# Retention and a feed-forward block on one core: queries loaded with four tokens on a partition, outputs scaled in the order of the result, and keys 6 transposed by the DMA queue

## The chip, the cores and the metric

The kernel runs on one core of one Trainium2 chip. The metric is the device time of one execution in microseconds (us), from the runs' own clock; the profile is taken in an execution of its own, and its span, from the first to the last instruction, is a little shorter.

A core has a matrix engine (TensorE; PE in the profile, PEld for its weight loads), three engines for elementwise work (VectorE = DVE, ScalarE = ACT, GpSimd = POOL), and a queue engine (SyncE = SP) that here issues nearly all DMA transfers. Sixteen DMA engines carry them out. SBUF is the memory on the core, PSUM the memory that TensorE writes its products into.

## The reference

The first half is a recurrent form of attention over a sequence of 768 tokens, for 4 batches and 8 heads of 64; its result goes through a feed-forward block with a product in the middle.

```python
# q, k, v: (4, 8, 768, 64)
gamma = 1 - 2 ** (-5 - arange(H))              # one decay for each head
for t in range(S):
    state = gamma * state + k[t] v[t]^T         # 64 x 64 for each batch and head
    y[t]  = scale * q[t] @ state
x = y.transpose(0, 2, 1, 3).reshape(B * S, H * D)        # (3072, 512)
a = x @ w1;  b = x @ w2                                  # (3072, 1024)
out = ((a * b) @ w3) @ w_out                             # (3072, 512)
```

## The kernel before

The work is cut into 12 steps, `m` = 0 to 11. A step takes 128 tokens (a chunk) of two batches; six chunks make up a sequence, so steps 0 to 5 belong to the first two batches and 6 to 11 to the other two. In a chunk the two halves of 64 tokens are `s` = 0 and 1. The heads come in four pairs `p`, with `r` for the head in the pair and `e` for the batch. Steps 0 and 1 have a form of their own (class `Pairs`), in which each of the two takes 256 tokens of one batch.

For each step the kernel multiplies keys by queries (`scores`), masks the result, multiplies it by the values (`intra`), adds the product of the queries with the state (`inter`), scales the sum by the decays (`outputs_back`), and carries the state on (`kv`). Step `m` also runs the feed-forward block of `m - 1` and its last product for `m - 2`. w3 and w_out have been multiplied into one matrix at the start.

TensorE needs queries and keys with the 64 elements of a head on the partitions. They come from memory with tokens on the partitions, are cast to 16 bits, and are then transposed, either by TensorE with a copy out of PSUM (`k_transposes`) or by a DMA transpose (`k_dma`, `q_dma`).

```python
wstage = ctx.enter_context(tc.tile_pool(name="wstage", bufs=22))
ps_f   = ctx.enter_context(tc.tile_pool(name="ps_f", bufs=4, space=PSUM))

def load_q(n):                         # 256 tokens of one batch, all heads
    g, e = divmod(n, 2)
    if g >= NSTEP // 2:
        return
    bp, cp = divmod(g, NCH // 2)
    q_in[n] = load_pairs(q, bp * 2 + e, cp)

def load_pairs(src, b, cp):            # two tokens on a partition: runs of 2 x 64 x 4 bytes
    t = new_stage()
    dma_in(
        t[:, :].rearrange("p (h x) -> p h x", x=2 * D),
        src[b, :, cp * 2 * C : (cp + 1) * 2 * C, :].rearrange("h (p t) d -> p h (t d)", t=2),
    )
    return t
...
def pairs_cast(dst, src, *engs):
    n = H // len(engs)
    for i, eng in enumerate(engs):
        hs = slice(i * n, i * n + n)
        (nc.scalar.copy if eng is nc.scalar else eng.tensor_copy)(
            dst[:, :].rearrange("i (t h d) -> i h t d", t=2, d=D)[:, hs, :, :],
            src[:, :].rearrange("i (h t d) -> i h t d", t=2, d=D)[:, hs, :, :],
        )
...
def q_dma(n):
    qT = att.tile([128, 2, NP, 128], HP, tag="qT", name="qT", bufs=5)
    nc.sync.dma_start_transpose(
        qT[:, :, :, :].rearrange("p t a i -> p (t a) i"), q16s.pop(n)[:, :]
    )
    qTs[n] = qT

def k_transposes(m, tag):              # eight transposes on TensorE, one copy on VectorE
    k16, kT = k16s[m], new_kT(m)
    ...
    for e in range(2):
        for p in range(NP):
            nc.tensor.transpose(ps[:, e, p, :], k16[:, e, p * 128 : (p + 1) * 128], ident16[:, :])
    nc.vector.tensor_copy(kT..., ps...)

def k_dma(m):
    nc.sync.dma_start_transpose(new_kT(m)..., k16s[m]...)

def queries(m, e, p, s, r):
    c = m % NCH
    i0 = c % 2 * 64 + s * 32
    return qTs[m // 2 * 2 + e][half(r), :, p, i0 : i0 + 32]      # 2 runs of 32 columns

def scores(m, engs=None):
    ...
                    nc.tensor.matmul(
                        ps[r][half(s), p * 2 + e, :], lhsT=kT[half(r), e, p, half(s)],
                        rhs=queries(m, e, p, s, r), start=True, stop=True,
                    )
    def back(r):                       # "am_back": the mask, on VectorE
        nc.vector.tensor_tensor(
            am[:, r, :, :], ps[r][:, :, :],
            keep[:, :].unsqueeze(1).broadcast_to((128, NP * 2, L)), MULT,
        )
...
def ended(mm, eng=None):               # a tiny copy that ends after mm
    mark = (eng.tensor_copy if eng else nc.scalar.copy)(mark_t[:, :], Z[0:1, 0:1])
    wait_for(mark, mm)
    return mark

def outputs_back(m, s):                # XT = psY * YS, tokens in natural order in XT
    swap = s == 1 and m % NCH > 0
    for to in (half(0), half(1)) if swap else (slice(0, 128),):
        fr = half(1 - to.start // L) if swap else to
        n = fr.stop - fr.start
        nc.vector.tensor_tensor(
            XT[m][to, :, s, :].rearrange("p (a e) (i t) -> p a e t i", e=2, t=2),
            psYs[m][s][fr, :, :].rearrange("p (a e) (t i) -> p a e t i", e=2, t=2),
            YS[fr, s + swap, :, :].unsqueeze(2).broadcast_to((n, NP, 2, L))
            .rearrange("p a e (t i) -> p a e t i", t=2),
            MULT,
        )
```

The products in PSUM have their 64 columns in the order of the query columns, all tokens with t = 0 first and then those with t = 1; XT has them in the order of the tokens.

The steps from 3 on, in the order in which each engine is given its instructions:

```python
EARLY = (6, 11, 12)        # intra(m - 1) already in step m - 1
K_PE = (3, 5)              # steps in which the next keys are transposed by TensorE

def step(m):
    kv_backs = []
    if m > 4:
        last = None if m in EARLY else ended(intra(m - 1))
        if m < NSTEP:
            kv_backs.append(kv(m, True))
            am_back = scores(m)
        inter(m - 1, last)
    ...
    outputs_back(m - 1, 0)
    outputs_back(m - 1, 1)
    if m >= NSTEP:
        return
    if m + 1 < NSTEP:
        k_cast(m + 1, (nc.gpsimd, nc.gpsimd))
        if m not in K_PE:
            k_dma(m + 1)
    for kv_back in kv_backs:
        kv_back(0)
        kv_back(1)
    am_back(0)
    am_back(1)
    ffn[m - 2].o_unit(0)               # 8 products of 512 columns each, and the store
    ffn[m - 2].o_unit(1)
    load_q(m + 3) if m % 2 == 0 else None
    load_k(m + 2)
    load_v(m + 2)
    load_q(m + 3) if m % 2 else None
    for f in range(2):
        ffn[m - 1].ab(f)               # 8 products of 256 columns, ScalarE copies a, VectorE multiplies
    if m + 1 in EARLY:
        intra(m)
    if m + 1 < NSTEP:
        v_cast(m + 1, (nc.gpsimd, nc.gpsimd))
    ...
    ffn[m - 1].ab(2)
    ffn[m - 1].ab(3)
    ...
    if m % 2 == 0:
        for n in (m + 2, m + 3):
            q_cast(n, nc.gpsimd)
        for n in (m + 2, m + 3):
            q_dma(n)
    for f in range(4, 8):
        if f == 6 and m in K_PE:
            k_transposes(m + 1, None)
        ffn[m - 1].ab(f)
```

Of the kernel before, what the change touches and what calls it, by code (L numbers as in the profile page):

```python
# [12 lines left out]
MULT = mybir.AluOpType.mult  # L13
# [5 lines left out]
def kernel(  # L19
# [11 lines left out]
    nc = tc.nc  # L31
    B, H, S, D = q.shape
    C = 128
    L = 64
    WST = 22
    NCH = S // C
# [4 lines left out]
    TB = 256  # L41
    K_PE = 4

# [15 lines left out]
    def half(x):  # L59
        return slice(x * L, (x + 1) * L)  # L60

    def dma_in(dst, src):
        nc.sync.dma_start(dst, src)  # L63
# [5 lines left out]
    q_in, k_in, v_in = {}, {}, {}  # L69

    def load_q(n):

        g, e = divmod(n, 2)
        if g >= NSTEP // 2:
            return
        bp, cp = divmod(g, NCH // 2)
        q_in[n] = load_pairs(q, bp * 2 + e, cp)

    def load_pairs(src, b, cp):
        t = new_stage()  # L80
# [5 lines that stand above are left out]
# [19 lines left out]
    def new_stage():  # L105
        return wstage.tile([128, 1024], FP, tag="wst", name="stg")
# [18 lines left out]
    for f in range(4, 8):  # L125
        w3_st.append(load_rows(moe_w3, f))
    for e in range(2):
        load_q(e)
        k_in[e] = load_pairs(k, e, 0)
        v_in[e] = load_pairs(v, e, 0)  # L130
    w1_st = [load_rows(moe_w1, d) for d in range(4)]
# [19 lines left out]
    for s in range(2):  # L151
        nc.gpsimd.iota(ip_i[half(s), 0:2, :], pattern=[[1, 2], [0, H]], base=1, channel_multiplier=2)
    if_i = const.tile([128, 2, L], mybir.dt.int32, name="if_i")
    nc.gpsimd.iota(if_i[:, :, :], pattern=[[L, 2], [1, 2], [2, 32]], base=1, channel_multiplier=0)
    LGH = const.tile([128, H], FP, name="LGH")
    LGP = const.tile([128, 2, NP], FP, name="LGP")
    for h in range(H):
# [2 lines left out]
    YS = const.tile([128, 3, NP, L], FP, name="YS")  # L160
# [12 lines left out]
    def masks_and_decays():  # L173

        nc.gpsimd.memset(keep[:, :], 1.0)
        for s in range(2):
            r = slice(s * L, (s + 1) * L)
            nc.gpsimd.affine_select(
                out=keep[r, :], in_=keep[r, :], compare_op=mybir.AluOpType.is_ge, fill=0.0,
                base=0, pattern=[[1, 2], [2, 32]], channel_multiplier=-1,  # L180
            )

        nc.gpsimd.memset(keep_t[:, :, :], 1.0)
        for s in range(2):
            for t in range(2):
                nc.gpsimd.affine_select(
                    out=keep_t[half(s), t, :], in_=keep_t[half(s), t, :], compare_op=mybir.AluOpType.is_ge,
                    fill=0.0, base=-t, pattern=[[1, 2], [2, 64]], channel_multiplier=-2,
                )
        for h in range(H):  # L190
            for s in range(2):
                nc.gpsimd.memset(LGP[half((h + s) % 2), s, h // 2 : h // 2 + 1], math.log(gam[h]))
        for h in range(H):
            p, r = h // 2, (h % 2) * 64
            nc.gpsimd.memset(GS[r : r + 64, p : p + 1], gam[h] ** C)
# [11 lines left out]
    XT = {}  # L207
# [70 lines left out]
    q16s, k16s, v16s, qTs, kTs, AMs, psYs, Ts = {}, {}, {}, {}, {}, {}, {}, {}  # L278

    def q_cast(n, *engs):  # L280
        if n not in q_in:
            return
        q16s[n] = att.tile([128, 1024], HP, tag="q16", name="q16", bufs=2)
        pairs_cast(q16s[n], q_in.pop(n), *engs)

    def pairs_cast(dst, src, *engs):
        n = H // len(engs)
        for i, eng in enumerate(engs):
            hs = slice(i * n, i * n + n)
            (nc.scalar.copy if eng is nc.scalar else eng.tensor_copy)(  # L290
                dst[:, :].rearrange("i (t h d) -> i h t d", t=2, d=D)[:, hs, :, :],
                src[:, :].rearrange("i (h t d) -> i h t d", t=2, d=D)[:, hs, :, :],
            )

    def k_cast(m, engs):
        k16 = att.tile([128, 2, 512], HP, tag="k16", name="k16", bufs=3)
        k32 = k_in.pop(m)
        if len(engs) == 1:
            parts = [(k16[:, :, :].rearrange("p e x -> p (e x)"), k32[:, :, :].rearrange("p e x -> p (e x)"))]
        else:  # L300
            parts = [(k16[:, e, :], k32[:, e, :]) for e in range(2)]
        for eng, (dst, src) in zip(engs, parts):
            (nc.scalar.copy if eng is nc.scalar else eng.tensor_copy)(dst, src)  # L303
        k16s[m] = k16
# [57 lines left out]
    def k_dma(m):  # L362
        nc.sync.dma_start_transpose(
            new_kT(m)[:, :, :, :].rearrange("p e a j -> p (e a) j"),
            k16s[m][:, :, :].rearrange("p e x -> p (e x)"),
        )

    def queries(m, e, p, s, r):
        c = m % NCH
        i0 = c % 2 * 64 + s * 32  # L370
        return qTs[m // 2 * 2 + e][half(r), :, p, i0 : i0 + 32]

# [22 lines left out]
    class Pairs:  # L397
# [4 lines left out]

        def k_cast(self, *engs):
            self.k16 = att.tile([128, 1024], HP, tag="k16", name="k16", bufs=3)
            pairs_cast(self.k16, k_in.pop(self.e), *engs)

        def k_transposes(self, tag, on_dve, parts=1):
            self.kT = att.tile([128, 2, NP, 128], HP, tag="kT", name="kT", bufs=2)
# [9 lines left out]
            )  # L418

        def queries(self, r, p, s):  # L420
            return qTs[self.e][half(r), :, p, half(s)]

        def scores(self, t):
            am = att.tile([128, 2, NP, 128], HP, tag="am", name="am")
# [18 lines left out]
        def intra(self, t):  # L443
            if t == 0:
                self.y = [bank(f"Y{s}", [128, NP, 128], FP, "psY") for s in range(2)]
            for p in range(NP):
                for s in range(2):
                    for r in range(2):
                        c0 = p * 128 + r * 64
                        last = nc.tensor.matmul(  # L450
                            self.y[s][half(r), p, :], lhsT=self.v16[half(s), t, c0 : c0 + 64],
                            rhs=self.am[t][half(s), r, p, :], start=(t == 0 and p == 0),
                            stop=(s == 0 and t == 1 and p == NP - 1),
                        )
            return last
# [50 lines left out]
        def outputs_back(self, s):  # L506
            if self.e not in XT:
                XT[self.e] = xpool.tile([128, NP * 2, 2, L], HP, tag="xt", name="xt")
            nc.vector.tensor_tensor(
                XT[self.e][:, :, :, :].rearrange("p (a s) b x -> p a s (b x)", s=2)[:, :, s, :]  # L510
                .rearrange("p a (b i t) -> p a t b i", b=2, t=2),
                self.y[s][:, :, :].rearrange("p a (t b i) -> p a t b i", t=2, b=2),
                YS[:, 0:2, :, :].rearrange("p b a (t i) -> p a t b i", t=2), MULT,
            )


# [68 lines left out]
    def ended(mm, eng=None):  # L585
# [4 lines that stand above are left out]
# [17 lines left out]
    def outputs_back(m, s):  # L607
        if m not in XT:
            XT[m] = xpool.tile([128, NP * 2, 2, L], HP, tag="xt", name="xt")
        swap = s == 1 and m % NCH > 0  # L610
        for to in (half(0), half(1)) if swap else (slice(0, 128),):
            fr = half(1 - to.start // L) if swap else to
            n = fr.stop - fr.start
            nc.vector.tensor_tensor(  # L614
                XT[m][to, :, s, :].rearrange("p (a e) (i t) -> p a e t i", e=2, t=2),
                psYs[m][s][fr, :, :].rearrange("p (a e) (t i) -> p a e t i", e=2, t=2),
                YS[fr, s + swap, :, :].unsqueeze(2).broadcast_to((n, NP, 2, L))
                .rearrange("p a e (t i) -> p a e t i", t=2),
                MULT,
            )  # L620

# [89 lines left out]
    w3_part(2, 1, 2)  # L711
    cast_wo(3)
    masks_and_decays()
    cast_w3(4)
    for f in range(3):
# [12 lines left out]
    wb.mm(4)  # L728
    wb.back()
    q_cast(0, nc.gpsimd)  # L730
    wb = W3Block(5)
    wb.mm(4)
# [22 lines left out]
    am_back(1)  # L755
    b0.intra(0)
    q_cast(1, nc.scalar, nc.gpsimd)
    wb.mm(1)
    q_transposes(1, "X0", False)
# [81 lines left out]
    q_cast(3, nc.gpsimd)  # L841
    q_transposes(2, "X0", False)
    k_cast(2, (nc.gpsimd, nc.scalar))
    v_cast(2, (nc.gpsimd, nc.gpsimd))
    for f in range(2):
# [27 lines left out]

    EARLY = (6, 11, 12)

    K_PE = (3, 5)

    def step(m):  # L880

# [4 lines that stand above are left out]
# [12 lines left out]
# [4 lines that stand above are left out]
# [11 lines left out]
# [4 lines that stand above are left out]
# [15 lines left out]
# [3 lines that stand above are left out]
# [43 lines left out]
```

## Time and profile before

| | before |
|---|---|
| time, median of 3 runs | 184.48 us (184.39 to 185.63) |
| span of the profiled execution | 181.5 us |
| TensorE busy | 175.3 us |
| VectorE busy | 108.6 us |
| ScalarE, GpSimd busy | 71.9, 71.3 us |
| DMA packets, data | 79,531, 39.71 MB |

The page of a profile gives the busy time of each engine and a row of 40 slices of the span, each digit the busy share in tenths. The chain of work that ended last follows back from the last instruction what released each piece of work, so that its pieces fill the span. Groups of instructions bear the line of the kernel that issued them (L614 is line 614), their shapes, the busy time, and the mean duration of one. A line with SPq is the time in which the queue engine was issuing a transfer, not the transfer itself; "to landing" is the time from an issue to the arrival of its data.

### The profile page before, as it was taken

The numbers are of one execution on the slowest core, as the hardware profiler recorded it, in microseconds if no ns is written. First come the engines' busy times: TensorE is split into PE (matmuls) and PEld (weight loads), VectorE is DVE, ScalarE is ACT, GpSimd is POOL, SyncE is SP. The second block draws the span as 40 slices with busy tenths as digits, with TensorE's granted clock in tenths as the row PEclk, the third lists the DMA queues.
The fourth block names the chain that finished last, engine by engine and source line by source line (L and its number), as shares of the span: only waits on it lengthen the run. The fifth ranks groups of instructions, "written<-read, shape, count | busy, mean of one in ns | idle before, by whom it ended". The sixth has DMA issues, their size and how long they took to land.

```text
span 181.5 us, 6220 instructions
## 1 busy us (share of the span) xinstructions
PE 175.3 (97%) x2634; PEld 125.4 (69%) x2634; DVE 108.6 (60%) x204; ACT 71.9 (40%) x156; POOL 71.3 (39%) x127
## 2 busy tenths in 40 slices
PE   7889999999999999999999999999999999999992
PEld 2445656688766785876967858768688587685871
DVE  1246658751769669558477584494674956745430
ACT  3354845555631341524334424244243332442431
POOL 3127536964537752725427273055460350000000
PEclk9999999999999999999999999999999999999999
DMA  5999999999999999999999999999999940201203
GB/s 204 376 417 401 298 291 350 409 371 242 194 256 226 182 301 211 203 312 198 245 202 198 295 169 244 190 208 265 236 114 261 178 149 4 116 0 42 78 0 116
DMA packets 79531, 39.71 MB, mean 219 GB/s; under 512 B 57361, under 2 KB 74001, under 8 KB 79505
## 3 DMA queue, kind: packets, MB, share of 16 engines
q1 hardware_dynamic: 79072, 38.81, 88.6%
q8 instruction: 20, 0.33, 0.8%
q10 hardware_dynamic: 432, 0.52, 0.8%
q14 instruction: 7, 0.05, 0.1%
HBM read 29.36 MB, written 6.29 MB: 196 GB/s over the span
## 4 chain that ended last, share of the span: by engine, by line
PE 88%; DMA 5%; ACT 2%; SPq 1%; DVE 1%; issue 0%; ACTq 0%
PE psF L636 41%; PE psO L663 23%; DMA stg<-in_moe_w_out_dram 5%; PE psF L795 4%; PE psW L269 3%; PE psW L255 3%; PE psY L531 2%; PE psY L599 2%; PE psA L383 2%; PE psG L636 2%; PE psK L551 2%; PE psTq L328 1%; PE psW L244 1%; SPq L63 1%; PE psTk L357 1%; PE psY L450 1%
## 5 line engine op out<-in xcount | busy, mean ns | idle before, releaser
L636 PE MATMUL psF<-xt,w 128*128 128x256 f16 x672 | 76.7, 273 | 0.0
L636 PEld LDWEIGHTS <-w 128*128 128x128 f16 x704 | 68.4, 98 | 10.3
L651 DVE TENSOR_TENSOR ht<-pa,psF 128x256 f16<-128x256 f32 x88 | 36.9, 420 | 37.6 <-PE psF L636 32.0
L645 ACT COPY pa<-psF 128x256 f32<-128x256 f32 x80 | 29.8, 373 | 37.5 <-PE psF L636 37.5
L663 PE MATMUL psO<-w3o,ht 128*128 128x512 f16 (+2 forms) x200 | 43.9, 371 | 0.0
L667 ACT ACTIVATE osb<-psO 128x512 f32<-128x512 f32 (+2 forms) x25 | 14.5, 581 | 44.0 <-PE psO L663 44.0
L663 PEld LDWEIGHTS <-ht 128*128 128x128 f16 x200 | 18.5, 98 | 19.4
L614 DVE TENSOR_TENSOR xt<-psY,YS 64x512 f16<-64x512 f32 (+1 forms) x29 | 21.1, 727 | 4.8 <-PE psY L599 4.4
L310 POOL TENSOR_TENSOR v<-stg,VS 128x512 f16<-128x512 f32 x20 | 20.6, 1042 | 5.4 <-DMA stg<-in_v_dram 5.4
L303 POOL CAST k<-stg 128x512 f16<-128x512 f32 x18 | 11.0, 612 | 26.1 <-DMA stg<-in_k_dram 25.9
L290 POOL CAST q<-stg 128x1024 f16<-128x1024 f32 (+1 forms) x12 | 12.0, 1003 | 17.9 <-DMA stg<-in_q_dram 13.8
L390 DVE TENSOR_TENSOR am<-psA,keep 128x512 f16<-128x512 f32 x20 | 12.8, 682 | 0.6 <-PE psA L383 0.6
L566 POOL TENSOR_TENSOR t<-s,GS 128x512 f16<-128x512 f32 x8 | 8.3, 1039 | 7.8 <-DVE s L565 7.8
L248 DVE COPY w3t<-psW 128x1024 f16<-128x1024 f16 x8 | 5.5, 690 | 5.3 <-PE psW L244 5.3
L269 PE MATMUL psW<-wo,w3t 128*128 128x512 f16 x32 | 8.6, 381 | 0.0
L255 PE MATMUL psW<-wo,w3t 128*128 128x512 f16 x32 | 8.0, 387 | 0.7 <-ACT wo L224 0.5
L795 PE MATMUL psF<-xt,w 128*128 128x256 f16 x64 | 8.3, 273 | 0.2
L686 PE MATMUL psZ<-zeros 128*128 128x512 f16 (+1 forms) x18 | 6.6, 504 | 1.3 <-DVE zeros L143 1.3
L795 PEld LDWEIGHTS <-w 128*128 128x128 f16 x64 | 5.8, 98 | 1.8 <-ACT w L769 0.6
L573 DVE TENSOR_TENSOR t<-psK,t 128x512 f16<-128x512 f32 x9 | 6.2, 690 | 0.6 <-PE psK L551 0.5
L244 PEld LDWEIGHTS <-w3h 128*128 128x128 f16 x64 | 4.4, 103 | 3.1 <-DVE w3h L231 1.7
L225 POOL CAST wo<-stg 128x512 f16<-128x512 f32 x4 | 2.5, 613 | 10.2 <-DMA stg<-in_moe_w_out_dram 10.2
(92 smaller groups left out, 149.3 us busy)
## 6 DMA issues: line engine op xcount, KB each, us to landing
stg<-in_moe_w_dram SPq DMA_DIRECT2D x16, 512.0 KB, 8.8
stg<-in_q_dram SPq DMA_DIRECT2D x12, 512.0 KB, 6.4
out_dram<-osb SPq DMA_DIRECT2D x22, 256.0 KB, 3.3
stg<-in_k_dram SPq DMA_DIRECT2D x20, 256.0 KB, 5.6
stg<-in_v_dram SPq DMA_DIRECT2D x20, 256.0 KB, 5.6
stg<-in_moe_w_out_dram SPq DMA_DIRECT2D x4, 512.0 KB, 7.9
stg<-in_k_dram SPq DMA_DIRECT2D x2, 512.0 KB, 9.5
stg<-in_v_dram SPq DMA_DIRECT2D x2, 512.0 KB, 8.6
```

The source lines that it names most:

```text
L255: nc.tensor.matmul(acc[f], lhsT=w3t[f][:, g * 128 : (g + 1) * 128], rhs=WO[i][:, r, :], start=(g == 0), stop=(g == 7),)
L269: nc.tensor.matmul(self.ps[:, :], lhsT=self.t[:, g * 128 : (g + 1) * 128], rhs=WO[g // 2][:, g % 2, :], start=(g == 0), stop=(g == 7),)
L290: (nc.scalar.copy if eng is nc.scalar else eng.tensor_copy)(dst[:, :].rearrange("i (t h d) -> i h t d", t=2, d=D)[:, hs, :, :], src[:, :]. ...
L310: eng.tensor_tensor(v16[:, e, :].rearrange("j (h d) -> j h d", d=D), v32[:, e, :].rearrange("j (h d) -> j h d", d=D), VS[:, 2, :].unsqueez ...
L390: nc.vector.tensor_tensor(am[:, r, :, :], ps[r][:, :, :], keep[:, :].unsqueeze(1).broadcast_to((128, NP * 2, L)), MULT,)
L614: nc.vector.tensor_tensor(XT[m][to, :, s, :].rearrange("p (a e) (i t) -> p a e t i", e=2, t=2), psYs[m][s][fr, :, :].rearrange("p (a e) (t ...
L636: nc.tensor.matmul(ps[:, :], lhsT=W[d][:, f * 128 : (f + 1) * 128], rhs=self.x(d), start=(d == 0), stop=(d == 3),)
L645: nc.scalar.copy(self.pa[f][:, :], ps[:, :])
L651: nc.vector.tensor_tensor(self.HT[:, f, :], self.pa.pop(f)[:, :], ps[:, :], MULT)
L663: nc.tensor.matmul(psO[:, :], lhsT=self.HT[:, f, e * 128 : (e + 1) * 128], rhs=W3O[f][:, cs], start=(f == 0), stop=(f == 7),)
L667: nc.scalar.activation(osb[:, cs], psO[:, :], AF.Copy, scale=final_scale)
L795: nc.tensor.matmul(ps[f // 2][:, f % 2, :], lhsT=W[d][:, f * 128 : (f + 1) * 128], rhs=f0.x(d), start=(d == 0 and f % 2 == 0), stop=(d == ...
```

## The change

There are three parts to it. Queries of steps 2 to 11 are loaded with four tokens on a partition instead of two, so that a run in memory is 1,024 bytes long instead of 512. A tile then holds four heads of both batches, 64 partitions each, and is loaded by two transfers of half the size. The cast, the masks and the query columns follow this order: a product's 64 columns now are 4 runs of 16. Steps 0 and 1 keep loading two tokens on a partition, and take their query columns with a step of two so that they come in the same order.

Second, `outputs_back` goes through its elements in the order of the result (i, then t): XT and the decays are now gone through without gaps, and the products in PSUM with a step of 16 elements from one to the next. Before, it went through the products without gaps, and wrote XT with a step of two.

Third, the keys of step 6 are transposed by the DMA queue in step 5, where TensorE did it before; and the early `intra` is that of step 7 (in step 7, ahead of step 8) in place of that of step 10 (ahead of step 11). The aim of the change is to take work from TensorE's list, with room for it in the DMA engines made by longer runs.

```diff
--- before.py
+++ after.py
@@ -70,11 +70,17 @@
 
     def load_q(n):
 
-        g, e = divmod(n, 2)
+        g, hh = divmod(n, 2)
         if g >= NSTEP // 2:
             return
         bp, cp = divmod(g, NCH // 2)
-        q_in[n] = load_pairs(q, bp * 2 + e, cp)
+        q_in[n] = new_stage()
+        for e in range(2):
+            dma_in(
+                q_in[n][half(e), :].rearrange("p (h x) -> p h x", h=4),
+                q[bp * 2 + e, hh * 4 : hh * 4 + 4, cp * 2 * C : (cp + 1) * 2 * C, :]
+                .rearrange("h (p t) d -> p h (t d)", t=4),
+            )
 
     def load_pairs(src, b, cp):
         t = new_stage()
@@ -125,7 +131,7 @@
     for f in range(4, 8):
         w3_st.append(load_rows(moe_w3, f))
     for e in range(2):
-        load_q(e)
+        q_in[e] = load_pairs(q, e, 0)
         k_in[e] = load_pairs(k, e, 0)
         v_in[e] = load_pairs(v, e, 0)
     w1_st = [load_rows(moe_w1, d) for d in range(4)]
@@ -151,7 +157,7 @@
     for s in range(2):
         nc.gpsimd.iota(ip_i[half(s), 0:2, :], pattern=[[1, 2], [0, H]], base=1, channel_multiplier=2)
     if_i = const.tile([128, 2, L], mybir.dt.int32, name="if_i")
-    nc.gpsimd.iota(if_i[:, :, :], pattern=[[L, 2], [1, 2], [2, 32]], base=1, channel_multiplier=0)
+    nc.gpsimd.iota(if_i[:, :, :], pattern=[[L, 2], [1, L]], base=1, channel_multiplier=0)
     LGH = const.tile([128, H], FP, name="LGH")
     LGP = const.tile([128, 2, NP], FP, name="LGP")
     for h in range(H):
@@ -177,7 +183,7 @@
             r = slice(s * L, (s + 1) * L)
             nc.gpsimd.affine_select(
                 out=keep[r, :], in_=keep[r, :], compare_op=mybir.AluOpType.is_ge, fill=0.0,
-                base=0, pattern=[[1, 2], [2, 32]], channel_multiplier=-1,
+                base=0, pattern=[[1, 4], [4, 16]], channel_multiplier=-1,
             )
 
         nc.gpsimd.memset(keep_t[:, :, :], 1.0)
@@ -185,7 +191,7 @@
             for t in range(2):
                 nc.gpsimd.affine_select(
                     out=keep_t[half(s), t, :], in_=keep_t[half(s), t, :], compare_op=mybir.AluOpType.is_ge,
-                    fill=0.0, base=-t, pattern=[[1, 2], [2, 64]], channel_multiplier=-2,
+                    fill=0.0, base=-t, pattern=[[1, 4], [4, 32]], channel_multiplier=-2,
                 )
         for h in range(H):
             for s in range(2):
@@ -281,15 +287,15 @@
         if n not in q_in:
             return
         q16s[n] = att.tile([128, 1024], HP, tag="q16", name="q16", bufs=2)
-        pairs_cast(q16s[n], q_in.pop(n), *engs)
-
-    def pairs_cast(dst, src, *engs):
-        n = H // len(engs)
+        token_cast(q16s[n], q_in.pop(n), 2 if n < 2 else 4, *engs)
+
+    def token_cast(dst, src, t, *engs):
+        n = 1024 // D // t // len(engs)
         for i, eng in enumerate(engs):
             hs = slice(i * n, i * n + n)
             (nc.scalar.copy if eng is nc.scalar else eng.tensor_copy)(
-                dst[:, :].rearrange("i (t h d) -> i h t d", t=2, d=D)[:, hs, :, :],
-                src[:, :].rearrange("i (h t d) -> i h t d", t=2, d=D)[:, hs, :, :],
+                dst[:, :].rearrange("i (t h d) -> i h t d", t=t, d=D)[:, hs, :, :],
+                src[:, :].rearrange("i (h t d) -> i h t d", t=t, d=D)[:, hs, :, :],
             )
 
     def k_cast(m, engs):
@@ -366,9 +372,9 @@
         )
 
     def queries(m, e, p, s, r):
-        c = m % NCH
-        i0 = c % 2 * 64 + s * 32
-        return qTs[m // 2 * 2 + e][half(r), :, p, i0 : i0 + 32]
+        qT = qTs[m // 2 * 2 + p // 2][half(r), :, :, :].rearrange("p t a i -> p (t a) i")
+        i0 = e * 64 + m % NCH % 2 * 32 + s * 16
+        return qT[:, p % 2 : 8 : 2, i0 : i0 + 16]
 
 
 
@@ -402,7 +408,7 @@
 
         def k_cast(self, *engs):
             self.k16 = att.tile([128, 1024], HP, tag="k16", name="k16", bufs=3)
-            pairs_cast(self.k16, k_in.pop(self.e), *engs)
+            token_cast(self.k16, k_in.pop(self.e), 2, *engs)
 
         def k_transposes(self, tag, on_dve, parts=1):
             self.kT = att.tile([128, 2, NP, 128], HP, tag="kT", name="kT", bufs=2)
@@ -418,7 +424,7 @@
             )
 
         def queries(self, r, p, s):
-            return qTs[self.e][half(r), :, p, half(s)]
+            return qTs[self.e][half(r), :, p, half(s)].rearrange("d t (i u) -> d u t i", u=2)
 
         def scores(self, t):
             am = att.tile([128, 2, NP, 128], HP, tag="am", name="am")
@@ -508,9 +514,9 @@
                 XT[self.e] = xpool.tile([128, NP * 2, 2, L], HP, tag="xt", name="xt")
             nc.vector.tensor_tensor(
                 XT[self.e][:, :, :, :].rearrange("p (a s) b x -> p a s (b x)", s=2)[:, :, s, :]
-                .rearrange("p a (b i t) -> p a t b i", b=2, t=2),
-                self.y[s][:, :, :].rearrange("p a (t b i) -> p a t b i", t=2, b=2),
-                YS[:, 0:2, :, :].rearrange("p b a (t i) -> p a t b i", t=2), MULT,
+                .rearrange("p a (b i t) -> p a b i t", b=2, t=4),
+                self.y[s][:, :, :].rearrange("p a (t b i) -> p a b i t", t=4, b=2),
+                YS[:, 0:2, :, :].rearrange("p b a (i t) -> p a b i t", t=4), MULT,
             )
 
 
@@ -612,10 +618,10 @@
             fr = half(1 - to.start // L) if swap else to
             n = fr.stop - fr.start
             nc.vector.tensor_tensor(
-                XT[m][to, :, s, :].rearrange("p (a e) (i t) -> p a e t i", e=2, t=2),
-                psYs[m][s][fr, :, :].rearrange("p (a e) (t i) -> p a e t i", e=2, t=2),
+                XT[m][to, :, s, :].rearrange("p (a e) (i t) -> p a e i t", e=2, t=4),
+                psYs[m][s][fr, :, :].rearrange("p (a e) (t i) -> p a e i t", e=2, t=4),
                 YS[fr, s + swap, :, :].unsqueeze(2).broadcast_to((n, NP, 2, L))
-                .rearrange("p a e (t i) -> p a e t i", t=2),
+                .rearrange("p a e (i t) -> p a e i t", t=4),
                 MULT,
             )
 
@@ -873,9 +879,9 @@
 
 
 
-    EARLY = (6, 11, 12)
-
-    K_PE = (3, 5)
+    EARLY = (6, 8, 12)
+
+    K_PE = (3,)
 
     def step(m):
```

## The prediction

> **What bounds the kernel now.** I read the page first, for the engine that is full; then the chain of waits, to see what that engine does from one end of a step to the other; then the groups of VectorE by shape, the time lines of the engines around step 5, and the DMA issues.
>
> From the page (busy share, then 40 slices of the span):
>
> ```profile
> PE 175.3 (97%) x2634; PEld 125.4 (69%) x2634; DVE 108.6 (60%) x204; ACT 71.9 (40%) x156; POOL 71.3 (39%) x127
> ...
> PE   7889999999999999999999999999999999999992
> ...
> PEclk9999999999999999999999999999999999999999
> DMA  5999999999999999999999999999999940201203
> ```
>
> TensorE is full from the fourth slice to the last, at full clock. The DMA engines are full too until the 33rd slice, so a second bound stands close behind. Which of them ends the waits is told by the chain, here around step 5 (start, length, what; steps count from 0):
>
> ```profile
> 79.67 0.38 PE psY L531 x32
> ...
> 86.54 3.60 PE psF L636 x32
> 90.14 0.45 PE psTk L357 x8
> 90.58 1.75 PE psF L636 x16
> 92.33 0.37 PE psK L551 x32
> 92.70 0.29 PE psA L383 x32
> 93.00 0.29 PE psY L599 x32
> 93.29 3.56 PE psO L663 x16
> ```
>
> Each piece starts where the one before ends: TensorE waits for nothing here, and the same is true of the whole chain from 42.9 to 177.5 us, but for 0.10 us in step 8. A projection of 64 products of 256 columns takes 6.99 us, 109 ns each. So the time is the sum of TensorE's work, plus a start of some 12.5 us (the chain's 8.69 us of waiting for the first output weights lie in it) and 3.5 us behind the last product. A change is worth what it takes from TensorE's list, less any new wait of TensorE. In this stretch the list has one item that the change removes: the eight transposes of keys 6, 0.45 us.
>
> [...]
> [...] 512 columns out of PSUM, written without gaps, take 682 ns (L390 below). [...]
> [...] no instruction in this trace reads PSUM with a hop. This is my largest doubt.
> [...] The query columns go from runs of 64 bytes to runs of 32[...]; in the first two blocks they get a step of 4 bytes[...]. The trace can't test it.
> [...] 55,296 packets of 256 bytes took 24.4 ns in the mean, 16,384 of 512 bytes 31.0, 2,816 of 2,048 bytes 95.8.
>
> **Part 1, keys 6 by the queue.** Removed: eight transposes on TensorE, 0.45 us on the path, and VectorE's copy of them (L358, 0.69 us), off the path. Added: one DMA transpose, 1,024 packets of 256 bytes, 1024 x 24.4 ns / 16 = 1.6 us of all DMA engines. It goes behind the two query transposes of step 5 in the queue. The queue's own time line:
>
> ```profile
> 82.54 4.23 SPq L340 DMA_TRANSPOSE qT<-q  x2
> 86.86 1.02 SPq L669 DMA_DIRECT2D out_dram<-osb  x2
> ...
> 104.70 4.74 SPq L340 DMA_TRANSPOSE qT<-q  x2
> 109.54 1.30 SPq L363 DMA_TRANSPOSE kT<-k  x1
> ```
>
> Its input is ready: the second half of keys 6 is cast at 84.06 to 84.67 us. So it is issued at about 86.8. The same sequence of three stands in step 7 (104.70 and 109.54), where the key transpose landed 3.2 us after its issue; the DMA issues give over all
>
> ```profile
> kT<-k SPq DMA_TRANSPOSE x6, 4.6
> ```
>
> with 3.2 to 5.3 us as the extremes. It therefore lands between 90.0 and 92.1, in the middle at 91.4. TensorE asks for it at the scores of step 6: 92.70 less the 0.45 removed, 92.25. Slack 0.1 to 2.2 us, in the middle 0.85. It should be in time, barely. The stores and loads behind it move back by 1.3 to 2.6 us of issue. Keys 7, cast at 93.1 to 94.8, would be issued for transposition at up to 97 and land at 102; their scores are at 104.32 - 0.45 = 103.9. That too holds. Keys 8 are tighter: issued at 109.54, landed at 112.7, wanted at 115.8; 2 us of delay leave 1 us.
>
> **Part 2, queries with four tokens.** Ten of the twelve query tiles come in 512 packets of 1,024 bytes instead of 1,024 of 512. Between the measured sizes I interpolate 52 ns for 1,024 bytes: 512 x 52 / 16 = 1.7 us against 1024 x 31.0 / 16 = 2.0 us, so 0.3 us a tile and 3 us of DMA time in all, about twice what part 1 adds. That widens the slack of part 1 and takes nothing from TensorE by itself. Each load is now two issues; at 0.45 us for one the queue has room. GpSimd's query casts keep 1,024 elements (1,038 ns each). TensorE's scores and inter products keep number and shape.
>
> **Part 3, outputs scaled in the order of the result.** VectorE's groups (busy us, mean ns):
>
> ```profile
> L614 DVE TENSOR_TENSOR xt<-psY,YS 64x512 f16<-64x512 f32 x18 | 13.1, 726 | 0.2
> L390 DVE TENSOR_TENSOR am<-psA,keep 128x512 f16<-128x512 f32 x20 | 12.8, 682 | 0.6 <-PE psA L383 0.6
> L614 DVE TENSOR_TENSOR xt<-psY,YS 128x512 f16<-128x512 f32 x11 | 8.0, 728 | 4.5 <-PE psY L599 4.4
> ```
>
> L614 writes with gaps now and takes 45 ns more than L390, which doesn't. In the new order it writes without gaps and reads PSUM with a hop of 16 words at each element instead. If the hop is free, 33 of them save 33 x 45 ns = 1.5 us of VectorE, off the path. [...]
>
> **Part 4, the early intra products** go from step 11 to step 8. The number of products is the same. The 0.10 us wait in step 8 goes; the like of it may come in step 11, whose key-value products are half as many and hide ScalarE's marker less. I count 0.
>
> **Sum.** -0.45 us on TensorE, nothing else on the path: 184.48 - 0.45 = 184.0 us.
>
> **The rivals.**
> *VectorE becomes the bound by the hop* (28%). [...] Against it: VectorE takes only one element in about 1.02 ns here anyway (682 ns for 512 columns, 420 for the 256 of L651), and the new order looks chosen over gaps of 8 bytes in the writes. What it makes of the time is read from VectorE's list at the start of step 8:
>
> ```profile
> 117.24 2.20 DVE L614 TENSOR_TENSOR xt<-psY,YS 128x512 f16<-128x512 f32 x3 [1.08 <-PE psY L599]
> 119.47 0.69 DVE L573 TENSOR_TENSOR t<-psK,t 128x512 f16<-128x512 f32 x1
> 120.20 0.69 DVE L565 TENSOR_TENSOR s<-psK,t 128x512 f32<-128x512 f32 x1
> 120.81 1.28 DVE L390 TENSOR_TENSOR am<-psA,keep 128x512 f16<-128x512 f32 x2
> 122.00 0.41 DVE L651 TENSOR_TENSOR ht<-pa,psF 128x256 f16<-128x256 f32 x1
> ```
>
> The outputs are wanted by TensorE at 120.72 and ready at 119.44, 1.3 us of slack. [...]
>
> *The key transpose comes late* (15%). It takes the place of the work removed: scores 6, or 8, wait. One of them late by up to 1 us gives 184 to 185.
>
> *Shorter query runs slow TensorE's reads* (5%). If scores and inter products went from 0.3 to 0.45 us each, 18 such groups would add 2.7 us: 186.7.
>
> *The lighter DMA shortens more than that* (10%). Only the waits before 42.9 us could shrink, but the first loads of queries are as before and the weights stand ahead of the others. At most a few tenths: 183.6.
>
> **Range and chances.** The middle case has a bit over half of the weight and lies at 184.0, with the scatter of the runs before (184.39 to 185.63) around it. Low end 183.3: everything fits and a few tenths come on top. High end 187.0[...]. Faster by over 2% means below 180.8, which would need 3.7 us off TensorE's list; nothing in the change removes that: 1%. Slower by over 2% means above 188.2[...]: 8%. Within 2%: 91%.
>
> **What would show it.** Right: eight transposes fewer in the chain's step 5 and no piece that isn't TensorE from 43 us on; the span shorter by about 0.45 us; seven DMA transposes of keys, the new one landed before the scores of step 6; 512-byte packets down by 10,240; L614's successor at about 682 ns. Wrong: that group at 1 us or more, and products of L651 waited for by TensorE at the start of steps 8 to 10; or a wait of the score's weight loads for keys 6 or 8; or score groups of the chain well above 0.3 us.

## The result and the profile after

| | before | after |
|---|---|---|
| time, median of 4 runs | 185.0 us (184.39 to 185.63) | 191.06 us (190.8 to 191.33) |
| ratio, 95% interval | | 1.0327 [1.028, 1.0374] |
| span of the profiled execution | 181.5 us | 189.2 us |
| DMA packets, data | 79,531, 39.71 MB | 75,626, 39.97 MB |

The change makes the kernel 3.3% slower. (The medians of before lie between 183.4 and 185.0 us from one batch of runs to another; below, each experiment is compared with runs of before on the same chip, by ratio.) The spans differ by 7.7 us and the medians by 6.1, because the profiled execution of before (183.27 us) was faster than all four runs of before in the table, and that of the change (191.33 us) was the slowest of its four; losses read from the two chains are therefore somewhat larger than that of the medians. Lines of the changed kernel are some 6 higher than before, so that L614 is now L620, L383 is L389, and so on.

The page of the changed kernel, busy share and slices:

```profile
PE 175.6 (93%) x2626; PEld 124.2 (66%) x2626; DVE 106.9 (57%) x203; ACT 71.8 (38%) x156; POOL 71.6 (38%) x127
...
PE   7889999996799799999979999889998999999993
...
DMA  5999999999799899999999999999999965110202
```

TensorE has the same 175 us of work in a longer span, and its row has dips where it had none. So nothing was added to its list; it waits. Its waits, summed by what it waited for (total us, times, longest):

```profile
PE psA L389 <- DMA kT<-k: 2.8, 2, 1.5
...
PE psO L669 <- issue: 1.2, 1, 1.2
PE psTq L334 <- POOL q L296: 1.1, 1, 1.1
...
PE psF L642 <- issue: 0.9, 2, 0.6
```

The same view of the kernel before has none of these four. Where the time is lost can be dated by the chains, at the same piece of work in both: the transposes of queries 2 start at 48.08 us instead of 45.71 (+2.4), the last products of step 4 at 73.42 instead of 69.12 (+4.3), those of step 6 at 98.54 instead of 93.29 (+5.3), those of step 8 at 124.52 instead of 117.16 (+7.4), and from there to the end it stays at +7.3 to +8.1. The chain of before has, at the transposes of queries 2 (start, length, what),

```profile
45.71 0.45 PE psTq L328 x8
```

and the chain of the changed kernel shows the first of these losses and that around keys 6:

```profile
33.39 13.44 DMA stg<-in_q_dram
...
46.98 1.05 POOL q L296
...
48.08 0.63 PE psTq L334 x8
...
88.00 6.50 DMA stg<-in_v_dram
...
94.56 0.09 POOL v L316
94.66 3.13 DMA kT<-k
...
97.83 0.45 PE psA L389 x32
98.28 0.26 PE psY L605 x30
98.54 3.56 PE psO L669 x16
```

A chain that was all TensorE from 42.9 us on now runs through loads of queries, values and keys. The new key transpose itself is quick, 3.13 us from issue to landing. It is issued at 94.66, though, 7.8 us later than worked out. The queue's time line of the changed kernel shows it behind the two query transposes, which start at 90.26 instead of 82.54:

```profile
90.26 4.23 SPq L346 DMA_TRANSPOSE qT<-q  x2
94.66 1.24 SPq L369 DMA_TRANSPOSE kT<-k  x1
```

The inputs of all three came late. GpSimd's time line, first a line of before, then the changed kernel (start, length, what, idle before):

```profile
81.69 1.04 POOL L290 CAST q<-stg 128x1024 f16<-128x1024 f32 x1 [3.45 <-DMA stg<-in_q_dram]
```

```profile
88.85 1.04 POOL L296 CAST q<-stg 128x1024 f16<-128x1024 f32 x1 [4.43 <-DMA stg<-in_q_dram]
90.76 0.62 POOL L309 CAST k<-stg 128x512 f16<-128x512 f32 x1 [0.87 <-DMA stg<-in_k_dram]
91.78 0.62 POOL L309 CAST k<-stg 128x512 f16<-128x512 f32 x1 [0.41 <-DMA stg<-in_k_dram]
```

The second cast of queries ran at 81.69 before and runs at 88.85 here, after 4.43 us of waiting for the load instead of 3.45; the keys are cast behind it, until 92.4. So the query loads, which were to become cheaper, are slower. The packet records say by how much (a packet is the piece in which the records count what the DMA engines move; the ten new query tiles are 5,120 packets, one for each run):

| mean duration of a packet | before | after |
|---|---|---|
| 256 bytes (keys, values, transposes) | 24.4 ns | 25.7 ns |
| 512 bytes (the query loads of before among them) | 31.0 ns | 32.0 ns |
| 1,024 bytes (the new query loads) | | 75.2 ns |
| 2,048 bytes | 95.8 ns | 91.1 ns |

VectorE's outputs, where I had my largest doubt, are fine; its groups in the changed kernel:

```profile
L620 DVE TENSOR_TENSOR xt<-psY,YS 64x512 f16<-64x512 f32 x18 | 12.4, 688 | 0.2
L620 DVE TENSOR_TENSOR xt<-psY,YS 128x512 f16<-128x512 f32 x11 | 7.6, 689 | 7.3 <-PE psY L605 7.3
```

They take 688 ns instead of 727.

### The profile page after: what moved, and what is told of

Same layout as the page of the kernel before. It is cut to its first block, busy times and chain, and to the rows that moved or that the text cites. A ratio compares the mean times of both kernels' runs of the same rounds, so it can differ in the third digit from the quotient of the medians.

```text
span 189.2 us, 6220 instructions
## 1 busy us (share of the span) xinstructions
PE 175.6 (93%) x2626; PEld 124.2 (66%) x2626; DVE 106.9 (57%) x203; ACT 71.8 (38%) x156; POOL 71.6 (38%) x127
## 2 busy tenths in 40 slices
DMA packets 75626, 39.97 MB, mean 211 GB/s; under 512 B 58576, under 2 KB 70096, under 8 KB 75600
## 4 chain that ended last, share of the span: by engine, by line
PE 53%; DMA 26%; SPq 13%; issue 3%; POOL 3%; ACT 1%; ACTq 0%; POOLq 0%
PE psF L642 28%; PE psO L669 19%; SPq L63 12%; DMA stg<-in_q_dram 10%; DMA stg<-in_moe_w_out_dram 5%; DMA kT<-k 4%; DMA stg<-in_moe_w_dram 3%; DMA stg<-in_v_dram 3%; PE psA L389 2%; PE psY L605 1%; PE psY L537 1%; POOL q L296 1%; PE psK L557 1%; PE psTk L363 1%; PE psTq L334 1%
## 5 line engine op out<-in xcount | busy, mean ns | idle before, releaser
L620 DVE TENSOR_TENSOR xt<-psY,YS 64x512 f16<-64x512 f32 (+1 forms) x29 | 20.0, 688 | 7.5 <-PE psY L605 7.3
L389 PE MATMUL psA<-qT,kT 64*64 64x64 f16 x320 | 4.7, 195 | 2.8 <-DMA kT<-k 2.8
```

Of the source, the lines that this page charges most:

```text
L620: nc.vector.tensor_tensor(XT[m][to, :, s, :].rearrange("p (a e) (i t) -> p a e i t", e=2, t=4), psYs[m][s][fr, :, :].rearrange("p (a e) (t ...
```

## The experiments

The theory (H): a query tile is now loaded by two transfers, one for partitions 0 to 63 and one for 64 to 127, and the packets of a transfer that fills 64 neighbouring partitions take longer than those of one over all 128. At this point it was an estimate of mine, from the 75.2 ns of the 1,024-byte packets where 52 was interpolated. Rivals: the added key transpose overloads the queue (K); two transfers in place of one cost by their number (N); runs of 1,024 bytes or the four-token order are slow of themselves (R).

### The third part alone

```diff
-    EARLY = (6, 11, 12)
+    EARLY = (6, 8, 12)
-    K_PE = (3, 5)
+    K_PE = (3,)
```

The base is the kernel before.

> The kernel before, with the third part of the change alone: keys 6 by the queue, early intra 8 in place of 11; query loads and output order as before. Theory H (the query loads in two halves of 64 partitions [...] take longer): this part is nearly harmless, 184.3 to 185.5 us, TensorE waiting 0 to 1 us for keys 6. Rival K (the seventh key transpose overloads the queue): most of the 6 us is here, 188 us or more, with waits at the scores of steps 6 and 8.

Measured: 1.0014 of before [0.9979, 1.005]. K falls. The chain of this kernel at step 6:

```profile
86.71 5.35 PE psF L636 x48
92.06 0.38 PE psK L551 x32
92.44 0.29 PE psA L383 x32
92.73 0.29 PE psY L599 x32
93.02 3.56 PE psO L663 x16
```

Keys 6 go to the queue at 87.38 us, land 4.1 us later, at 91.5, and are wanted at 92.44: in time by 0.9 us, TensorE doesn't wait. The part saves what it was to save: from the products of 512 columns in step 3 (the piece psO) to those of step 12 the chain takes 163.52 - 56.55 = 106.97 us, before 164.14 - 56.37 = 107.77. Of these 0.80 us, 0.45 are gone by step 6 (the eight transposes), the rest comes in steps 8 to 11. The same stretch took 107.44 us in two kernels further down that also keep the old third part (even and odd partitions; the order of the outputs alone), so that only some 0.45 us are shown to be the part's own. The median doesn't show them, because the start moves by as much from run to run: the psO piece of step 3 starts between 56.4 and 58.1 us in the kernels here that don't wait later on.

### The changed kernel without the third part

The same two lines undone in the changed kernel.

> The changed kernel without the third part: keys 6 by TensorE again, early intra 11. Theory H: still slow, 188.5 to 190.5 us: the 2.9 us lost before step 2 and the late loads stay, the waits for keys 6 (1.4 us) and part of that for keys 8 go. Rival K: 184.5 to 186 us.

Measured: 1.0287 [1.0201, 1.0372]. Most of the loss is in the other two parts. The 1,024-byte packets take 75.4 ns here too.

### Halves against even and odd partitions

Two kernels made from the kernel before, with two tokens on a partition and runs of 512 bytes as they were. Only the ten query loads from step 2 on are cut in two:

```diff
+    def load_cut(src, b, cp):
+        t = new_stage()
+        for x in range(2):
+            ps = half(x)                  # halves: 0-63 and 64-127
+            ps = slice(x, 128, 2)         # the other kernel: even and odd
+            dma_in(
+                t[ps, :].rearrange("p (h x) -> p h x", x=2 * D),
+                src[b, :, cp * 2 * C : (cp + 1) * 2 * C, :]
+                .rearrange("h (p t) d -> p h (t d)", t=2)[ps, :, :],
+            )
+        return t
```

> The kernel before, in which only the ten query loads from step 2 on are cut into two transfers, partitions 0 to 63 and 64 to 127; runs still of 512 bytes, everything else as before. Theory H: 187.5 to 190 us, and 512-byte packets that take some 45 to 60 ns instead of 31. Rival N (two transfers instead of one, whatever they cover): the same 187.5 to 190 us. Rival R (runs of 1,024 bytes are slow of themselves, 75 ns): 184.5 to 185.5 us, nothing lost.

> As the run with halves, but the two transfers take the even and the odd partitions, 64 each. Theory H: [...] 184.3 to 185.7 us, as before, and packets near 31 ns. Rival N, or 64 partitions in a transfer of themselves: 187.5 to 190 us.

Measured: halves 1.0339 [1.0237, 1.0441], even and odd 1.0001 [0.9975, 1.0027]. This separates the theories. The bytes, the packets and the number of transfers are the same in both; only which partitions a transfer fills is different, and with them which runs of memory it reads (the change to the next kernel leaves the memory side alone). Halves give the whole loss of the change without any of its other parts, even and odd none. N falls by the second, R isn't needed by the first. TensorE's waits with halves are those of the change (total us, times, longest):

```profile
PE psA L393 <- DMA kT<-k: 2.4, 2, 1.9
PE psTq L338 <- POOL q L300: 1.8, 2, 1.3
...
PE psO L673 <- issue: 0.9, 1, 0.9
PE psF L646 <- issue: 0.6, 1, 0.6
```

With even and odd partitions the wait for keys is gone, and one for queries is left, before step 2:

```profile
PE psTq L338 <- POOL q L300: 0.8, 3, 0.3
```

The DMA issues of the two kernels (median us from issue to landing), halves first:

```profile
stg<-in_q_dram SPq DMA_DIRECT2D x20, 256.0 KB, 5.7
```

```profile
stg<-in_q_dram SPq DMA_DIRECT2D x20, 256.0 KB, 4.8
```

The 512-byte packets took 38.7 ns with halves and 30.9 with even and odd. Of 16,384 of them 6,144 belong to loads that weren't cut; at 32.0 ns for these, as in the changed kernel, the cut ones took an estimated 43 ns. I had expected 45 to 60.

### The whole change on even and odd partitions

If H is right, the change can be mended by where the two batches lie. In the changed kernel:

```diff
-                q_in[n][half(e), :].rearrange("p (h x) -> p h x", h=4),
+                q_in[n][e:128:2, :].rearrange("p (h x) -> p h x", h=4),
-        i0 = e * 64 + m % NCH % 2 * 32 + s * 16
-        return qT[:, p % 2 : 8 : 2, i0 : i0 + 16]
+        i0 = m % NCH % 2 * 64 + s * 32 + e
+        return qT[:, p % 2 : 8 : 2, i0 : i0 + 31 : 2]
```

A query's columns are now taken with a step of two, and each transfer reads the same bytes of memory as in the changed kernel, in the same runs.

> The changed kernel whole, but the two batches of a query tile lie on the even and on the odd partitions instead of 0 to 63 and 64 to 127[...]; runs stay 1,024 bytes, and the query columns are taken with a step of two. Theory H: the loss goes away, 0.992 to 1.002 of before, 1,024-byte packets take about 45 to 55 ns instead of 75, and keys 6 come in time. Rival (something else in the four-token form is slow too, the columns or the long runs): 1.01 or more.

Measured: 0.9976 [0.9953, 0.9999]. The loss is gone; the kernel is as fast as before or a little faster, 0.24% with an interval that just leaves out 1. The 1,024-byte packets take 55.1 ns instead of 75.2, at the upper edge of what was expected. TensorE's waits of this kernel:

```profile
PE psF L801 <- ACT w L775: 1.5, 1, 1.5
PE psZ L692 <- DVE zeros L149: 1.3, 1, 1.3
PE psW L261 <- ACT wo L230: 0.3, 1, 0.3
PE psA L435 <- DVE am L442: 0.2, 1, 0.2
```

All of them belong to the start; none is for keys or queries. As the memory side of the loads is the same in both, and the order of tokens too, the difference to the changed kernel, 75.2 ns a packet against 55.1, comes with the partitions of SBUF that each load fills. From step 3 to step 12 the chain takes 164.24 - 57.28 = 106.96 us, like the third part alone. Beside the loads in halves other packets were slower too: the 56,320 packets of 256 bytes, of which both kernels have the same, took 25.7 ns in the changed kernel and 24.6 here. In time of the sixteen engines that is 3.9 us, beside 6.4 us for the query packets themselves.

### The same without the third part

> The same without the third part: keys 6 by TensorE, early intra 11. Theory H: within 0.5% of before, 0.995 to 1.003; the difference to the run with the third part is the 0.45 us of the eight transposes, if keys 6 come in time there. Rival: 1.01 or more.

Measured: 0.9978 [0.9953, 1.0004]. The four-token form on even and odd partitions costs nothing. The 0.45 us between this and the kernel above is below what the medians resolve.

### The order of the outputs alone

The base is the kernel before, two tokens.

```diff
-                XT[m][to, :, s, :].rearrange("p (a e) (i t) -> p a e t i", e=2, t=2),
-                psYs[m][s][fr, :, :].rearrange("p (a e) (t i) -> p a e t i", e=2, t=2),
+                XT[m][to, :, s, :].rearrange("p (a e) (i t) -> p a e i t", e=2, t=2),
+                psYs[m][s][fr, :, :].rearrange("p (a e) (t i) -> p a e i t", e=2, t=2),
```

The decays and the outputs of steps 0 and 1 likewise.

> The kernel before, with the second part alone: outputs scaled in the order of the result (two tokens, so the hop in PSUM is 32 words), all loads and transposes as before. By the trace of the changed kernel the hop is free: the scaling takes 688 ns instead of 727, and it is off the path, so 0.997 to 1.003. If the step of 32 words costs where that of 16 did not: 1,000 ns or more each, 1.005 to 1.02.

Measured: 0.9985 [0.9957, 1.0014], 688 ns each. The hop in PSUM costs no more at 32 words than at 16 (688 ns in the changed kernel), and the part is off the path.

### Keys 4 by the queue as well

The kernel on even and odd partitions with `K_PE = ()`.

> As the changed kernel with even and odd partitions, and keys 4 by the queue as well, so that no keys from step 3 on are transposed by TensorE. If the queue has room in step 3: another 0.45 us less than that run, 0.989 to 1.000. If not: TensorE waits for keys 4 at the scores of step 4, 1 to 3 us more, 1.00 to 1.01.

Measured: 0.9994 [0.9957, 1.0031], so not told apart from before by its time. In its chain step 3 to step 12 takes 163.49 - 56.85 = 106.64 us: 0.45 less by step 4, of which 0.12 is lost again by step 6. It is no clear step beyond the kernel above.

### Quarters, in two orders

Made from the kernel before: four transfers of 32 partitions, in order (0, 32, 64, 96) or alternating (0, 64, 32, 96).

```diff
+        for x in (0, 1, 2, 3):            # the other kernel: (0, 2, 1, 3)
+            ps = slice(x * 32, x * 32 + 32)
```

> The kernel before with the ten query loads cut into four transfers of 32 partitions in order: 0 to 31, 32 to 63, 64 to 95, 96 to 127. [...] this is the cut into halves again, with twice the transfers: 1.02 to 1.05 of before, 512-byte packets at 36 to 45 ns. If only the count of partitions in a transfer mattered, 32 would be worse than 64: over 1.05.

> The same four transfers in the order 0 to 31, 64 to 95, 32 to 63, 96 to 127[...]. If transfers that follow each other overlap in the DMA engines, part of the loss comes back: 1.00 to 1.02. If [...]: no difference to the run in order.

Measured: in order 1.0431 [1.0366, 1.0496], alternating 1.0364 [1.0299, 1.0428], packets of 512 bytes 38.3 and 36.3 ns. Alternating was to bring back part of the loss, 1.00 to 1.02, if transfers that follow each other overlap, and did not; the two intervals overlap, so that a small gain (the medians are 191.64 and 189.94 us) is neither shown nor excluded. Transfers that follow each other on different halves don't make up for the loss: 3.6% stays. The order is no remedy; a step of two partitions within each transfer is (1.0001).

## Why the prediction was wrong

**What bounds the kernel** was read rightly: TensorE's list, with the DMA engines close behind it. The warning was there, slices of 9 in the DMA row up to the 32nd, but they don't tell how close: before, even and odd and halves have nearly the same row. Two readings were loose and change nothing: behind the last product lie 4.0 us (181.5 - 177.5), not 3.5, and the 1.02 ns an element of VectorE is the slope between 256 and 512 columns, (682 - 420) / 256, not 682 / 512 = 1.33.

**Part 2 is the step that failed.** It held that a query tile would cost 512 x 52 / 16 = 1.7 us of DMA instead of 2.0, "about twice what part 1 adds", and so widen the slack. Measured: 512 x 75.2 / 16 = 2.4 us. For ten tiles that is 24.1 us against 19.8 before, 4.2 us more where the prediction had 3 us less. The packet size was not the error: on even and odd partitions the same packets take 55.1 ns, ten tiles 17.6 us, near the interpolated 52 ns (52.9 ns without the third part). The error was to see in the two transfers only the second issue ("the queue has room") and not which partitions they fill, though the diff has them in `half(e)`. The list of rivals lacked this one, so the range did too.

**Part 1** stands by itself. With the query loads as before, keys 6 landed 0.9 us ahead of their use, where the prediction had 0.1 to 2.2, in the middle 0.85. In the changed kernel "its input is ready" fell: the second half of keys 6 was cast at 91.78 to 92.4 us instead of 84.06 to 84.67, and the query transposes ahead of it in the queue were late by as much. The rival that had keys 6 or 8 late came true, by 1.3 and 1.5 us, but as a result of the late loads, and with two other losses that it didn't count: 2.4 us before step 2, and waits marked "issue".

**Part 3** was right: the scaling takes 688 ns, off the path. The rival with 28%, VectorE bound by the hop, falls; so does that of shorter query runs: with 16 columns in a run the scores of step 4 take 0.32 us in the chain, as before, and with a step of two columns as well the kernel is at 0.9976.

**Part 4** was put at 0, and no run shows it to be otherwise. Between steps 6 and 12 the chain of the third part alone is 0.35 us shorter than that of before, but with the early products as before this chain varies by more, from 107.44 to 108.02 us over steps 3 to 12.

**The sum** of -0.45 us fits the chain of the third part alone and was wrong for the whole: the measured +6 us comes with the term of the loads, since halves alone bring it and even and odd partitions take it away. The 4.2 us of their own packets don't add up to it; the slower packets of 256 bytes beside them are another part, and how much of TensorE's waits each of the two makes is not shown.

**Open:** why neighbouring partitions are slower. The loss goes by contiguous partitions (1.0339 in halves, 1.0431 and 1.0364 in quarters, 1.0001 on even and odd); the records name no DMA engine, and no run shows the cause. Open too are the waits marked "issue" (1.2 and 0.9 us in the changed kernel, 1.7 us at one place in that without the third part): they appear in the kernels with halves, and on even and odd partitions not at all in three of four kernels and with 0.3 us in the one without the third part, but not with quarters either, where loads are as late. What TensorE waits for in them the profile doesn't say, and no run tried it.

## What to carry to other kernels

When a load is cut, ask which partitions each piece fills, not only how long its runs are and how many pieces there are: halves of 64 neighbouring partitions cost 3.4% of the kernel here, even and odd partitions nothing (1.0001). Where two sources share a tile, lay them on alternating partitions and take the step out again where it cost nothing here, in the columns of a product (0.9976). And where the DMA row is full of nines, count each transfer's time in DMA engines before and after, by packets of the same size that also go to the same kind of partitions: the slack of everything that waits behind hangs on it (keys 6 were cast 7.7 us later here).

## What the runs showed that I had not expected

VectorE read PSUM with a hop of 16 or 32 words at each element almost as fast as without (512 columns in 688 ns; the masking, which reads without hops, takes 681), while writing 16-bit results with a step of two, and reading without hops, took 727, some 40 ns more. And a 256 KB load on 64 neighbouring partitions landed after 5.7 us in the median where one on every second partition took 4.8.
